# A SwiGLU kernel on one core: x rows 0 to 383 turned by a DMA copy, in place of 256 rows turned on TensorE

## The chip, the cores and the metric

The kernel runs on one core of one Trainium2 chip; the other seven cores are idle. The metric is the device time of one execution in microseconds (us), as the median of several runs. A profile of one execution goes with it: it lists what each engine did and when. The engines are TensorE (PE, with its weight loads as PEld), VectorE (DVE), ScalarE (ACT), GpSimd (POOL) and SyncE (SP). SP and ACT issue the DMA transfers here, each on a queue of its own.

## The reference

```python
B, S, D, F = 1, 2048, 640, 1536          # all bfloat16
def reference(x, w_gate, w_up, w_down):
    g = silu(x @ w_gate)                 # [2048, 1536]
    u = x @ w_up                         # [2048, 1536]
    return (g * u) @ w_down              # [2048, 640]
```

## The kernel before, in words

The 2048 rows of x are worked on in four blocks of 512 (`S_BLK`). A matmul contracts over the 128 partitions, so x has to stand with D on the partitions: `xT` holds it so, as 5 slices (kd) of 128 by 2048. `wg_sb` and `wu_sb` hold the two first weights, also as 5 slices; F is cut into 12 chunks of 128 (fc). For each block and each fc, the gate projection (`pg`) and the up projection (`pu`) are 5 matmuls each of up to 512 columns (`proj`, lines 192 to 203). ACT then takes the silu of `pg`, and DVE multiplies it by `pu` into `aT` (`gate`, lines 210 to 217). After the 12 chunks of a block the down projection follows: 12 matmuls for the last 128 columns of the output, turned back on DVE, and 4 x 12 matmuls for its first 512 columns (lines 258 to 308). The last four rows of x are worked out on DVE, spread over the later blocks, so that the last block has only 508 columns in its projections.

The change touches the head, which is block 0 with the first four fc (`EARLY = 4`). Its loads are issued in program order, and SP's instructions are kept in that order to the end (`keep_order`, line 315). Before:

- SP loads x rows 0 to 127 as they lie, ACT loads rows 128 to 255 (`load_x`, lines 111 and 112).
- The gate weights of the first four fc come in five slices of 128 KB, one for each kd (lines 113 to 117): kd 1 on ACT's queue, the others on SP's.
- Rows 256 to 511 are copied by `turn_x` (line 118), a DMA that turns the data through the crossbar on its way, so that they land in `xT` directly.
- Behind it SP issues the first two `wu_sb` loads of 320 KB (two fc each), then the rest of the gate and up weights, w_down, x rows 512 to 1023 by crossbar and more.

Meanwhile PE runs `N_WARM = 18` matmuls on a tile of ones, whose result isn't used (`warm`, line 174). It then turns the first 256 rows itself: 10 transposes of 128 by 128 against an identity (which POOL makes, line 71), copied out of PSUM by ACT and DVE (`transpose_chunk`, line 180). The gate matmuls of the head (lines 230 to 235) go kd by kd over all four fc, so that each needs only one slice of weights: first kd 0 in two steps of 128 columns, then kd 1 to 4 over columns 0 to 255 (`HALF`), then all five kd over columns 256 to 511. After them the four up projections of the head run, each 5 matmuls of 512 columns. PE's order in the head is fixed as written (line 241).

Of the kernel before, what the change touches and what calls it, by code (L numbers as in the profile page):

```python
# [7 lines left out]


@with_exitstack  # L10
def _body(
# [8 lines left out]
    nc = tc.nc  # L20
    P = nc.NUM_PARTITIONS
    f32 = mybir.dt.float32
    bf16 = mybir.dt.bfloat16
    ACT = mybir.ActivationFunctionType
    ALU = mybir.AluOpType

    B, S0, D = x.shape
    F = w_gate.shape[1]
    S = B * S0
    x2 = x.rearrange("b s d -> (b s) d")  # L30
    out2 = out.rearrange("b s d -> (b s) d")

    KD = D // P
    KF = F // P
    S_BLK = 512
    NSB = S // S_BLK
    SUB = S_BLK // P
    HALF = S_BLK // 2
    DA = 512
    Q = 32  # L40
    N_WARM = 18
    T = 4
    WT_STEP = 4
    ROW_J = 0
    EARLY = 4
# [3 lines left out]
    consts = ctx.enter_context(tc.tile_pool(name="consts", bufs=1))  # L49
    work = ctx.enter_context(tc.tile_pool(name="work", bufs=3))  # L50
    outp = ctx.enter_context(tc.tile_pool(name="outp", bufs=3))
    psum = ctx.enter_context(
        tc.tile_pool(name="psum", bufs=2, space=bass.MemoryType.PSUM)
    )

    ident = consts.tile([P, P], bf16)
    x_sb = consts.tile([P, HALF // P, D], bf16)
    xT = consts.tile([P, KD, S], bf16)
    wg_sb = consts.tile([P, KD, F], bf16)
    wu_sb = consts.tile([P, KD, F], bf16)  # L60
# [7 lines left out]
    row_s = consts.tile([P, KF, T], f32)  # L68
    prod = consts.tile([P, D], f32)

    make_identity(nc, ident[:])

    x_v = x2.rearrange("(c p) d -> p c d", p=P)
    xt_v = x2.rearrange("s (kd p) -> s kd p", p=P)
    wg_v = w_gate.rearrange("(kd p) f -> p kd f", p=P)
    wu_v = w_up.rearrange("(kd p) f -> p kd f", p=P)
# [2 lines left out]
    def wslice(a, b):  # L79
        return slice(a * P, b * P)  # L80

    def load_w(eng, dst, src, a, b):
        eng.dma_start(out=dst[:, :, wslice(a, b)], in_=src[:, :, wslice(a, b)])

    def load_x(eng, c0, c1):
        eng.dma_start(out=x_sb[:, c0:c1, :], in_=x_v[:, c0:c1, :])  # L86

    def issue_order(a, b):
        tc.add_manual_dep(
# [8 lines left out]
    def keep_order(engine):  # L98

        traced = [i for i in nc.cur_bb.bb.instructions if i.engine == engine]  # L100
        for a, b in zip(traced, traced[1:]):
            issue_order(a, b)

    def turn_x(r0, r1):
        nc.sync.dma_start_transpose(out=xT[:, :, r0:r1], in_=xt_v[r0:r1])

    ones = consts.tile([P, P], bf16)
    silu_first = consts.tile([P, 1], f32)
    nc.vector.memset(ones[:], 1.0)  # L109

    load_x(nc.sync, 0, 1)
    load_x(nc.scalar, 1, 2)
    for kd in range(KD):
        eng = nc.scalar if kd == 1 else nc.sync
        eng.dma_start(
            out=wg_sb[:, kd, wslice(0, EARLY)], in_=wg_v[:, kd, wslice(0, EARLY)]
        )
    turn_x(HALF, S_BLK)
    nc.scalar.activation(silu_first[:], ones[:, 0:1], ACT.Silu)  # L119
    for a in range(0, EARLY, 2):  # L120
        load_w(nc.sync, wu_sb, wu_v, a, a + 2)
    for a, b in W_CHUNKS:
# [6 lines left out]
    def turn_w(dst, src, f0, f1):  # L129
# [7 lines left out]
        out=x_row[:],  # L137
        in_=x2[S - T : S, :].rearrange("t d -> (t d)").partition_broadcast(P),
# [35 lines left out]
    def warm(n):  # L174
        for _ in range(n):
            nc.tensor.matmul(  # L176
                pw[:, 0:P], lhsT=ones[:], rhs=ones[:], start=True, stop=True
            )

    def transpose_chunk(c, parts):  # L180
        c_sl = slice(c * P, (c + 1) * P)
        for copy, tag, k0, k1 in parts:
            pt = psum.tile([P, k1 - k0, P], bf16, tag=tag, name="pt")
            for kd in range(k0, k1):
                nc.tensor.transpose(  # L185
                    out=pt[:, kd - k0, :],
                    in_=x_sb[:, c, kd * P : (kd + 1) * P],
                    identity=ident[:],
                )
            copy(out=xT[:, k0:k1, c_sl], in_=pt[:])  # L190

    def proj_step(ps, w_sb, fc, sb, c0, c1, kd):
        nc.tensor.matmul(  # L193
            ps[:, c0:c1],
            lhsT=w_sb[:, kd, fc * P : (fc + 1) * P],
            rhs=xT[:, kd, sb * S_BLK + c0 : sb * S_BLK + c1],
            start=(kd == 0 and c0 in (0, HALF)),
            stop=(kd == KD - 1),
        )

    def proj(ps, w_sb, fc, sb, c0, c1):
        for kd in range(KD):
            proj_step(ps, w_sb, fc, sb, c0, c1, kd)
# [6 lines left out]
    def gate(pg, pu, sb, fc, n_s):  # L210

        s0 = sb * S_BLK
        sg = work.tile([P, S_BLK], f32, name="sg")
        nc.scalar.activation(sg[:, 0:n_s], pg[:, 0:n_s], ACT.Silu)  # L214
        nc.vector.tensor_tensor(  # L215
            out=aT[:, fc, s0 : s0 + n_s], in0=sg[:, 0:n_s], in1=pu[:, 0:n_s], op=ALU.mult
        )

    def head():
        dve, act = nc.vector.tensor_copy, nc.scalar.copy  # L220
        split = [(act, "po_a", 0, 2), (dve, "po_b", 2, KD)]
        pgs = [
            psum.tile([P, S_BLK], f32, tag="gu", name="pg", bufs=4)
            for _ in range(EARLY)
        ]
        warm(N_WARM)
        for c in range(HALF // P):
            transpose_chunk(c, split)

        steps = [(0, 0, P), (0, P, HALF)]  # L230
        steps += [(kd, 0, HALF) for kd in range(1, KD)]
        steps += [(kd, HALF, S_BLK) for kd in range(KD)]
        for kd, c0, c1 in steps:
            for fc in range(EARLY):
                proj_step(pgs[fc], wg_sb, fc, 0, c0, c1, kd)

        for fc in range(EARLY):
            pu = psum.tile([P, S_BLK], f32, tag=("po_a", "po_b")[fc % 2], name="pu")
            proj(pu, wu_sb, fc, 0, 0, S_BLK)
            gate(pgs[fc], pu, 0, fc, S_BLK)  # L240
        keep_order(mybir.EngineType.PE)
        keep_order(mybir.EngineType.Activation)

    head()
    for sb in range(NSB):
        n_s = S_BLK if sb < NSB - 1 else S_BLK - T
# [26 lines left out]
        for q in range(P // Q):  # L273
            nc.scalar.dma_start(
                out=out2[
                    sb * S_BLK : sb * S_BLK + n_t, DA + q * Q : DA + (q + 1) * Q
                ].rearrange("(i r) c -> r i c", r=Q),
                in_=ot_q[q * Q : (q + 1) * Q, :].rearrange("r (i c) -> r i c", c=Q),
            )

        for j in range(SUB):
# [6 lines left out]
            for c0, c1, tag in cols:  # L288
# [14 lines left out]
                eng = nc.sync if c1 < D else nc.scalar  # L303
# [82 lines left out]
def kernel(tc, *args):  # L386
    _body(tc, *args)
    tc.close()
    tc.compile()
    _trim(tc.nc)  # L390
# [30 lines left out]
```

## Time and profile before

| | us |
|---|---|
| median of 3 runs | 163.65 |
| lowest, highest | 163.2, 164.01 |
| span of the profiled execution | 161.8 |
| PE busy in it | 159.4 |
| DVE busy | 111.0 |
| ACT busy | 42.6 |

The span runs from the first to the last instruction of the profiled execution. That execution has no device time of its own listed; the median of the runs is 1.85 us above its span. A row of the timeline gives start, length, engine, line, operation, tiles and count; SPq and ACTq are the queues of the engines that issue DMAs, and the length there is that of issuing, not of the transfer. "To landing" counts from the start of the issue to the last of the transfer's completion marks. A matmul's length in a row includes the time in the pipeline, so the spacing of many is taken instead. A row of windows has, for each engine, busy time and count of instructions, then the granted clock, the busy share of the DMA engines and GB/s.

### The profile page before, as it was taken

Reading aid. Unit: us, or ns where it says so; the run is one execution under the profiler, and the core shown is the slowest. Engines: PE = TensorE matmul, PEld = TensorE weight load, DVE = VectorE, ACT = ScalarE, POOL = GpSimd, SP = SyncE. Lnnn points to the kernel's source line nnn. Section 1 sums busy time; section 2 is a strip of 40 time slices with the busy share of each in tenths; the row PEclk is TensorE's granted clock in tenths of the full one; section 3 lists DMA queues with packets and bytes.
Section 4 is the critical chain, followed back from the end, with each engine's and each line's share of the span. In section 5 each row is a group of like instructions: output and inputs, shape, how many; then the busy total and the mean of one; then the engine's idle time right before and its main releaser. Section 6 shows DMA issues by size and latency. Waiting matters only on the chain.

```text
span 161.8 us, 2142 instructions
## 1 busy us (share of the span) xinstructions
PE 159.4 (99%) x808; PEld 77.6 (48%) x808; DVE 111.0 (69%) x250; ACT 42.6 (26%) x74; POOL 0.6 (0%) x6
## 2 busy tenths in 40 slices
PE   8999999999999999999999999999999999999995
PEld 7854444444444444444444444444444444445454
DVE  2034223599569999989919999979964999993001
ACT  5051222112222222211222322221214222222121
POOL 1000000000000000000000000000000000000000
PEclk9999999999999999999999999999999999999999
DMA  6999999934189999003110000000321000000312
GB/s 212 231 351 349 361 248 231 222 75 91 34 192 159 235 236 184 4 0 34 65 65 0 0 4 2 0 0 3 62 67 34 0 0 0 0 0 4 48 41 73
DMA packets 41961, 15.86 MB, mean 98 GB/s; under 512 B 33504, under 2 KB 41824, under 8 KB 41952
## 3 DMA queue, kind: packets, MB, share of 16 engines
q1 hardware_dynamic: 33584, 14.93, 37.0%
q10 hardware_dynamic: 8368, 0.80, 3.5%
q8 instruction: 6, 0.10, 0.3%
q14 instruction: 3, 0.02, 0.1%
HBM read 6.88 MB, written 2.62 MB: 59 GB/s over the span
## 4 chain that ended last, share of the span: by engine, by line
PE 97%; DMA 2%; SPq 0%; DVE 0%; issue 0%
PE pg L193 32%; PE pu L193 32%; PE po_a L291 26%; PE po_t L261 6%; DMA wg_sb<-in_w_gate_dram 2%; SPq L86 0%; DVE ot_b L302 0%
## 5 line engine op out<-in xcount | busy, mean ns | idle before, releaser
L193 PE MATMUL pg<-xT,wg_sb 128*128 128x512 bf16 (+3 forms) x264 | 59.8, 363 | 0.1
L193 PE MATMUL pu<-xT,wu_sb 128*128 128x512 bf16 (+1 forms) x240 | 59.1, 379 | 0.0
L215 DVE TENSOR_TENSOR aT<-sg,pu 128x512 bf16<-128x512 f32 (+1 forms) x48 | 32.7, 682 | 32.3 <-PE pu L193 32.3
L214 ACT ACTIVATE sg<-pg 128x512 f32<-128x512 f32 (+1 forms) x48 | 28.4, 597 | 71.2 <-PE pg L193 67.4
L291 PE MATMUL po_a<-wd_sb,aT 128*128 128x512 bf16 (+4 forms) x228 | 42.8, 348 | 0.0
L147 DVE SCALAR_TENSOR_TENSOR prod<-wgT,x_row 128x640 f32<-128x640 bf16 x48 | 39.4, 821 | 1.5 <-DMA wgT<-in_w_gate_dram 0.4
L147 DVE SCALAR_TENSOR_TENSOR prod<-wuT,x_row 128x640 f32<-128x640 bf16 x48 | 39.4, 821 | 1.0
L193 PEld LDWEIGHTS <-wg_sb 128*128 128x128 bf16 x264 | 25.9, 100 | 26.8 <-DMA wg_sb<-in_w_gate_dram 0.4
L193 PEld LDWEIGHTS <-wu_sb 128*128 128x128 bf16 x240 | 23.4, 98 | 28.1 <-DMA wu_sb<-in_w_up_dram 0.3
L291 PEld LDWEIGHTS <-aT 128*128 128x128 bf16 x228 | 20.8, 98 | 21.7
L300 ACT CAST ot<-po_a 128x512 bf16<-128x512 f32 (+2 forms) x17 | 9.5, 559 | 31.8 <-PE po_a L291 20.2
L261 PE MATMUL po_t<-aT,wd_sb 128*128 128x512 bf16 (+1 forms) x48 | 10.4, 366 | 0.0
L261 PEld LDWEIGHTS <-wd_sb 128*128 128x128 bf16 x48 | 4.7, 98 | 5.1
L302 DVE CAST ot_b<-po_a 128x96 bf16<-128x96 f32 (+1 forms) x2 | 0.5, 240 | 9.7 <-PE po_a L291 9.6
L270 ACT CAST ot_t<-po_t 128x512 bf16<-128x512 f32 (+1 forms) x4 | 2.2, 559 | 11.6 <-PE po_t L261 11.6
L147 DVE DVE_READ_ACCUMULATOR prod<-wgT,x_row 128x1 f32 x48 | 3.9, 82 | 0.0
L147 DVE DVE_READ_ACCUMULATOR prod<-wuT,x_row 128x1 f32 x48 | 3.9, 82 | 0.0
L272 DVE STREAM_TRANSPOSE ot_q<-ot_t 128x512 bf16<-128x512 bf16 (+1 forms) x4 | 2.7, 676 | 1.7 <-ACT ot_t L270 1.7
L190 DVE COPY xT<-pt 128x384 bf16<-128x384 bf16 x2 | 0.7, 358 | 2.9 <-PE pt L185 2.9
L176 PE MATMUL pw<-ones 128*128 128x128 bf16 x18 | 2.1, 313 | 0.4 <-DVE ones L109 0.4
L176 PEld LDWEIGHTS <-ones 128*128 128x128 bf16 x18 | 1.8, 147 | 0.4 <-DVE ones L109 0.4
L119 ACT ACT_TABLE_LOAD x1 | 1.3, 1283 | 1.0 <-issue 1.0
(13 smaller groups left out, 4.7 us busy)
## 6 DMA issues: line engine op xcount, KB each, us to landing
wd_sb<-in_w_down_dram SPq DMA_DIRECT2D x1, 1920.0 KB, 13.0
out_dram<-ot SPq DMA_DIRECT2D x15, 128.0 KB, 1.7
wg_sb<-in_w_gate_dram SPq DMA_DIRECT2D x2, 640.0 KB, 7.9
wu_sb<-in_w_up_dram SPq DMA_DIRECT2D x2, 640.0 KB, 8.6
wu_sb<-in_w_up_dram SPq DMA_DIRECT2D x2, 320.0 KB, 4.7
x_row<-in_x_dram SPq DMA_DIRECT2D x1, 640.0 KB, 5.1
wg_sb<-in_w_gate_dram SPq DMA_DIRECT2D x4, 128.0 KB, 3.4
out_dram<-ot_q ACTq DMA_DIRECT2D x12, 32.0 KB, 1.9
```

Source lines behind the costliest of these rows:

```text
L119: nc.scalar.activation(silu_first[:], ones[:, 0:1], ACT.Silu)
L147: nc.vector.scalar_tensor_tensor(out=prod[:], in0=wT[:, fc, :], scalar=1.0, in1=x_row[:, t, :], op0=ALU.mult, op1=ALU.mult, accum_out=acc[ ...
L176: nc.tensor.matmul(pw[:, 0:P], lhsT=ones[:], rhs=ones[:], start=True, stop=True)
L190: copy(out=xT[:, k0:k1, c_sl], in_=pt[:])
L193: nc.tensor.matmul(ps[:, c0:c1], lhsT=w_sb[:, kd, fc * P : (fc + 1) * P], rhs=xT[:, kd, sb * S_BLK + c0 : sb * S_BLK + c1], start=(kd == 0 ...
L214: nc.scalar.activation(sg[:, 0:n_s], pg[:, 0:n_s], ACT.Silu)
L215: nc.vector.tensor_tensor(out=aT[:, fc, s0 : s0 + n_s], in0=sg[:, 0:n_s], in1=pu[:, 0:n_s], op=ALU.mult)
L261: nc.tensor.matmul(po_t[:], lhsT=wd_sb[:, kf, DA:D], rhs=aT[:, kf, sb * S_BLK : sb * S_BLK + n_t], start=(kf == 0), stop=(kf == KF - 1),)
L270: nc.scalar.copy(ot_t[:], po_t[:])
L272: nc.vector.transpose(out=ot_q[:], in_=ot_t[:])
L291: nc.tensor.matmul(po[:], lhsT=aT[:, kf, s0 : s0 + P], rhs=wd_sb[:, kf, c0:c1], start=(kf == 0), stop=(kf == KF - 1),)
L300: nc.scalar.copy(ot[:], po[:])
```

## The change

Columns 0 to 383 of `xT` come by one crossbar copy, the very first DMA on SP. The five gate slices follow on SP's queue in three DMAs (kd 0; kd 1 and 2; kd 3 and 4), then the crossbar copy of rows 384 to 511, then the same loads as before. ACT issues no load in the head any more, and its first silu (which loads its table) is written ahead of the loads. The plain x loads, the identity, the transposes and their copies are gone. The head's gate matmuls are 20 of 384 columns and then 20 of 128, and 30 warm-up matmuls run in place of 18.

```diff
-    HALF = S_BLK // 2
+    HALF = 3 * P
-    N_WARM = 18
+    N_WARM = 30
...
-    ident = consts.tile([P, P], bf16)
-    x_sb = consts.tile([P, HALF // P, D], bf16)
...
-    make_identity(nc, ident[:])
...
-    load_x(nc.sync, 0, 1)
-    load_x(nc.scalar, 1, 2)
-    for kd in range(KD):
-        eng = nc.scalar if kd == 1 else nc.sync
+    def load_d(eng, k0, k1):
         eng.dma_start(
-            out=wg_sb[:, kd, wslice(0, EARLY)], in_=wg_v[:, kd, wslice(0, EARLY)]
-        )
+            out=wg_sb[:, k0:k1, wslice(0, EARLY)], in_=wg_v[:, k0:k1, wslice(0, EARLY)]
+        )
+
+    nc.scalar.activation(silu_first[:], ones[:, 0:1], ACT.Silu)
+    turn_x(0, HALF)
+    load_d(nc.sync, 0, 1)
+    load_d(nc.sync, 1, 3)
+    load_d(nc.sync, 3, KD)
     turn_x(HALF, S_BLK)
-    nc.scalar.activation(silu_first[:], ones[:, 0:1], ACT.Silu)
...
-    def transpose_chunk(c, parts):
...
     def head():
-        dve, act = nc.vector.tensor_copy, nc.scalar.copy
-        split = [(act, "po_a", 0, 2), (dve, "po_b", 2, KD)]
...
         warm(N_WARM)
-        for c in range(HALF // P):
-            transpose_chunk(c, split)
-
-        steps = [(0, 0, P), (0, P, HALF)]
-        steps += [(kd, 0, HALF) for kd in range(1, KD)]
+        steps = [(kd, 0, HALF) for kd in range(KD)]
         steps += [(kd, HALF, S_BLK) for kd in range(KD)]
```

More of the change, by code (lines that the diff above doesn't have):

```diff
@@ L6 @@
 from concourse._compat import with_exitstack
-from concourse.masks import make_identity
 @with_exitstack
@@ L69, in _body @@
     prod = consts.tile([P, D], f32)
-    make_identity(nc, ident[:])
-    x_v = x2.rearrange("(c p) d -> p c d", p=P)
     xt_v = x2.rearrange("s (kd p) -> s kd p", p=P)
@@ L83, in load_w @@
         eng.dma_start(out=dst[:, :, wslice(a, b)], in_=src[:, :, wslice(a, b)])
-    def load_x(eng, c0, c1):
-        eng.dma_start(out=x_sb[:, c0:c1, :], in_=x_v[:, c0:c1, :])
     def issue_order(a, b):
@@ L178, in warm @@
             )
-    def transpose_chunk(c, parts):
[L181 to L188, printed above, removed]
-                )
-            copy(out=xT[:, k0:k1, c_sl], in_=pt[:])
     def proj_step(ps, w_sb, fc, sb, c0, c1, kd):
```

## The prediction

> **What bounds the kernel now.** I read the page first, its first lines and its chain.
>
> ```profile
> span 161.8 us, 2142 instructions
> PE 159.4 (99%) x808; PEld 77.6 (48%) x808; DVE 111.0 (69%) x250; ACT 42.6 (26%) x74; POOL 0.6 (0%) x6
> ...
> PEclk9999999999999999999999999999999999999999
> ...
> PE 97%; DMA 2%; SPq 0%; DVE 0%; issue 0%
> ```
>
> TensorE is the bound from its first gate matmul to the end, and 97% of the chain is PE. Only the head, where DMA decides, can move. So next the chain in order of time (start, length, what; the last row is from the far end and serves as a price).
>
> ```profile
> 0.45 3.21 DMA wg_sb<-in_w_gate_dram
> ...
> 3.71 5.21 PE pg L193 x44
> 8.92 4.37 PE pu L193 x20
> 13.29 1.08 PE pg L193 x5
> 14.36 1.08 PE pu L193 x5
> ...
> 43.50 1.08 PE pg L193 x5
> ...
> 146.90 1.95 PE po_t L261 x12
> ```
>
> The first gate matmul starts at 3.71, when gate slice kd 0 has landed (0.45 + 3.21 = 3.66). From there on PE is handed from group to group with no wait in the chain. So the question is one number: when does the first up projection (`pu`) start after the change, and does anything behind it wait for DMA? The timeline gives that start, 8.79 (start, length, instruction, count).
>
> ```profile
> 0.39 2.10 PE L176 MATMUL pw<-ones 128*128 128x128 bf16 x18 [0.39 <-DVE ones L109]
> 2.31 1.25 PE L185 MATMUL pt<-ident,x_sb 128*128 128x128 bf16 x10
> 3.71 5.21 PE L193 MATMUL pg<-xT,wg_sb 128*128 128x128 bf16 x44
> 8.79 4.49 PE L193 MATMUL pu<-xT,wu_sb 128*128 128x512 bf16 x20
> ...
> 14.20 1.24 PE L193 MATMUL pu<-xT,wu_sb 128*128 128x512 bf16 x5
> ```
>
> These rows also price a matmul. Five 512-wide ones take 1.08 us in the chain (216 ns each), twelve 384-wide ones 1.95 (162.5 ns): 53.5 ns per 128 columns, so about 55 ns for 128 and 109 ns for 256. But the 18 warm-up matmuls, 128 wide, take 2.10 us: less some 0.3 for the last one's tail, that is 105 ns each, twice the later price. The first microseconds run at half clock, although the PEclk row shows 9 from the start. The 44 gate matmuls (8 of 128 and 36 of 256) would cost 8 x 55 + 36 x 109 = 4.36 us at the full rate; from 3.71 to 8.79 they took 5.08. Of the 0.72 over, I put about 0.6 down to a cold stretch until roughly 4.9 (1.2 us at half rate); the rest is small waits.
>
> **SP's queue and the landings.** First SP's issues, then landings (us from issue; two answers for single 320 KB and 640 KB loads), then the three copies by crossbar: 256 rows in the head, 512 rows at 44.58 and at 59.73.
>
> ```profile
> 0.00 0.39 SPq L86 DMA_DIRECT2D x_sb<-in_x_dram  x1
> 0.45 1.84 SPq L115 DMA_DIRECT2D wg_sb<-in_w_gate_dram  x4
> 2.33 1.91 SPq L105 DMA_TRANSPOSE xT<-in_x_dram  x1
> 4.29 1.15 SPq L83 DMA_DIRECT2D wu_sb<-in_w_up_dram  x2
> ...
> 6.06 0.92 SPq L83 DMA_DIRECT2D wu_sb<-in_w_up_dram  x1
> ...
> 11.83 11.46 SPq L105 DMA_TRANSPOSE xT<-in_x_dram  x1
> ...
> 44.58 2.73 SPq L105 DMA_TRANSPOSE xT<-in_x_dram  x1
> ...
> 59.73 3.22 SPq L105 DMA_TRANSPOSE xT<-in_x_dram  x1
> ```
>
> ```profile
> DMA to landing us min/median/max: 3.2/3.4/3.6
> ...
> wu_sb<-in_w_up_dram SPq DMA_DIRECT2D x1, 320.0 KB, 4.5
> wu_sb<-in_w_up_dram SPq DMA_DIRECT2D x1, 320.0 KB, 4.9
> wu_sb<-in_w_up_dram SPq DMA_DIRECT2D x1, 640.0 KB, 8.0
> ...
> out_dram<-ot SPq DMA_DIRECT2D x15, 128.0 KB, 1.7
> ```
>
> ```profile
> xT<-in_x_dram SPq DMA_TRANSPOSE x1, 4.2
> ...
> xT<-in_x_dram SPq DMA_TRANSPOSE x1, 5.4
> ...
> xT<-in_x_dram SPq DMA_TRANSPOSE x1, 5.2
> ```
>
> The first row of the second fence is the gate slices (128 KB each). The first `wu` load was issued at 4.29 and landed at 4.29 + 4.5 = 8.8, just when `pu` started: gates and load arrive together today. The 640 KB `wu` load for fc 4 to 7 was issued at 6.06 and landed at 14.0; its first user starts at 14.20. That is a cover of only 0.2 us.
>
> **The change, part by part.**
>
> *Removed.* The 10 transposes (1.25 us of PE), their four copies on DVE and ACT, the identity on POOL, the two plain x loads. All of it lay ahead of 3.71 and beside the gate slice that was waited for until 3.66, so none of it is saved as such. It does take away the PE work that filled 2.31 to 3.56. ACT's queue loses a gate slice, which goes to SP.
>
> *Warm-up, 18 to 30 matmuls.* At 107 ns (0.39 to 2.3 for 18) they are all issued by 0.39 + 30 x 0.107 = 3.6. They cost nothing as long as the first gate can't start before that, and it can't. What matters is the idle time behind them.
>
> *x rows 0-383 by crossbar, first on SP.* No row shows 384. Issue: 256 rows 1.91 us, 512 rows 2.73 to 3.22; I take 2.35. Landing: between 4.2 (256 rows) and 5.4 (512); I take the middle, 4.75. DMA rates give much the same. The windows below (last column GB/s) are plain loads in the head, then the first microsecond and the rest of the 512-row copy issued at 44.58.
>
> ```profile
> 2.00:3.00 1.00, 1.00 (x12) 0.92 (x11) 0.00 (x0) 0.77 (x3) 0.00 (x0) 1.00 0.95 315
> ...
> 45.80:46.80 1.00, 1.00 (x7) 0.41 (x6) 1.00 (x2) 0.02 (x1) 0.00 (x0) 1.00 0.89 165
> 46.80:48.50 1.70, 1.70 (x9) 0.78 (x8) 1.67 (x5) 0.57 (x1) 0.00 (x0) 1.00 1.24 275
> ```
>
> The 384 rows are 492 KB: 1 us at 165 and 1.2 us at 275. The data begin some 1.2 us after the issue (44.58 to 45.8), so they end near 3.4 to 3.6 and the semaphore comes later.
>
> The Trainium skill, page "Advanced Engine Details and Errata", section X-Bar Transpose (TRN2), calls such copies as fast as regular ones, 350 to 400 GB/s; by that figure 492 KB would take an estimated 1.2 to 1.4 us, the copy would land near 4.0 and the sum would fall to about +0.1. The rows just shown, 165 and then 275, speak against it here.
>
> *Gate slices behind it, all on SP.* kd 0 is issued at 2.40 instead of 0.45, kd 1-2 at 2.85, kd 3-4 at 3.4 (about 0.45 to 0.5 each, from 1.84 for four). Landing of kd 0: never sooner than 2.40 + 1.7 = 4.1 (the 128 KB store alone), at the latest 2.40 + 3.6 = 6.0. It lies behind the copy in the queue, and 128 KB at 315 GB/s is 0.4 us: 4.75 + 0.4 = 5.15. The other two have double size: 5.95 and 6.75.
>
> *Gates on 384 columns.* 20 x 162.5 ns = 3.25 and 20 x 55 ns = 1.10: 4.35, the same as the 4.36 above. At full clock: 5.15 + 0.65 = 5.80 (kd 0), wait to 5.95, + 1.30 = 7.25 (kd 1-2), + 1.30 = 8.55 (kd 3-4, landed by 6.75), + 1.10 = 9.65.
>
> *The copy of rows 384-511.* It is issued at 3.95. By the 256-row copy it lands no later than 3.95 + 4.2 = 8.15, and its first user is at 8.55: hidden by the 384-wide gates, cover 0.4. Its issue time is on the path, though: from 256 and 512 rows a straight line gives 1.3 to 1.5; in proportion it would be 1.0. I take 1.45.
>
> *What it is moved past.* The `wu` loads go from 4.29 to 5.45, and all later loads by as much. First `wu` chunk: 5.45 + 4.5 = 9.95 by today's row, 5.45 + 3.4 = 8.85 by the faster slices; today's waits behind a 256-row copy and will wait behind 128, so 4.2: 9.65, as late as the gates. Second chunk 6.0 + 4.9 = 10.9, wanted at 9.7 + 10 x 0.216 = 11.9. The 640 KB load moves with the stream, 14.0 + 0.9 = 14.9, against a use at 14.2 + 0.9 = 15.1: the 0.2 cover holds if DMA loses no more than PE. Behind that DMA has slack (the 512-row copy, issued at 11.83, isn't used before 43.5).
>
> **Sum.** `pu` starts at about 9.7 instead of 8.79: +0.9 us, and everything behind it moves by that. The span is 161.8 and the median of the runs 163.65; I carry the 1.85 between them unchanged: 164.55, say 164.6. Without a clock effect the change starts at +1.44 on the first gate (5.15 against 3.71) and gets about 0.6 back because its gates begin after the cold stretch.
>
> **Rivals.**
>
> *The clock is still cold (slower by more).* Before, PE works without a gap over 0.2 us from 0.39 on. After, it idles from 3.6 to about 5.15. If that gap spoils the release and the 4.5 us of work that preceded it in the old kernel (0.39 to 4.9) have to start again at 5.15, the gates run at half rate until 9.7: 14 of 384 (0.325 each) in that time, then 6 x 0.1625 + 1.10 = 2.1; `pu` at 11.8, +3.0 us, 166.6. If it is released halfway, +1.9. For it: the gap is new and long. Against it: more warm-up lies ahead of it. Chance 0.27.
>
> The Trainium skill, "TensorE: Matmul & The Clock Gate", section What's actually happening, has a free-running window of about 3.4 us that must be busy before the full clock is given; by that rule, with a window that ended near 4.9 in the old run, the same window would be some 60% busy (1.5 to 3.6), and if that is too little the next ends near 8.3: an estimated +2.5 us, 166.1. What share is enough the section doesn't say, and the trace only agrees that the first microseconds are slow.
>
> *Nothing lost (the other side).* Place: the queue behind the crossbar copy. If it lands at 4.2 like 256 rows and kd 0 follows at 4.4, the gates, warm and never waiting, end at 4.4 + 4.35 = 8.75, and `wu` at 8.85 decides: +0.1, 163.7. It decides from a first gate at 4.43 or earlier (8.79 - 4.35). For it: no other load is ahead of the copy now. Against: kd 0 can't pass it, and the 512-row copies took 5.2 and 5.4. Chance 0.20 for -0.4 to +0.5.
>
> *A real gain.* The runs of before spread from 163.2 to 164.0. If this comes from the moment of release, the old cold head may cost more than the 0.6 us of this profile in a typical run, while the new gates escape it. With one more microsecond of cold in the typical old run and the previous rival's landings it is -1 us, 162.7. Chance 0.10.
>
> **How the numbers follow.** The likeliest, 0.43, is +0.5 to +1.4, middle +0.9: 164.6, its own range 164.1 to 165.1. A measurement of this kernel can tell about 0.5% (0.82 us) from no change, and the likeliest lies on that border: 0.29 of its 0.43 above it. Slower: 0.29 + 0.27 = 0.56; same: 0.14 + 0.20 = 0.34; faster 0.10. The range runs from 163.2 (below nothing lost, by the spread) to 166.6 (clock fully lost); it leaves out the gain and a little above.
>
> **What would show it.** In the changed profile: SP's first copy about 2.35 us long and landing at 4.5 to 5; the first gate between 4.9 and 5.4, held by `wg_sb` and not by `xT`; its chain rows 4.35 us long plus a wait below 0.3; `pu` at 9.5 to 10; then a shift that is the same for the groups at 13.29 and 43.50 and at the end. A gate stage of 6 us or more without waits is the cold clock. A first gate under 4.5 is the second rival. Wrong in size: a `wu` load landing well after the gates' end, or a new wait near 15 on the 640 KB load.

## The result and the profile after

| | before | after |
|---|---|---|
| median of the runs | 163.64 us | 165.32 us |
| lowest, highest | 163.2, 165.71 | 163.88, 166.18 |
| span of the profiled execution | 161.8 | 162.6 |

The ratio of after to before is 1.0102, with a 95% interval of 1.0058 to 1.0147: slower by 1.7 us. The medians differ by more than the two profiles do (0.8 us). The profiled execution of after is the quickest of its six (163.88); three of the six lie at 163.9 to 164.7 and three at 165.9 to 166.2, and the median falls between them, where no run lies. So the profile shows one part of the loss only. Three disturbed executions, 165.71 of before and 166.56 and 168.6 of one kernel below, are left out of all ratios.

The page of after, first lines and chain:

```profile
span 162.6 us, 2114 instructions
PE 158.4 (97%) x794; PEld 76.5 (47%) x806; DVE 110.3 (68%) x248; ACT 41.9 (26%) x72; POOL 0.2 (0%) x4
...
PE 95%; DMA 2%; SPq 1%; issue 0%; DVE 0%
```

Its chain in order of time (start, length, what):

```profile
0.00 1.39 SPq L96
...
1.44 3.59 DMA wg_sb<-in_w_gate_dram
...
5.08 4.65 PE pg L174 x40
...
14.05 1.08 PE pg L174 x5
...
44.27 1.08 PE pg L174 x5
```

The chain still runs over the gate slice kd 0, which now is issued at 1.44 and lands at 5.04. The group of block 1 that stood at 43.50 stands at 44.27, 0.77 later. The timeline of after:

```profile
0.00 1.39 SPq L96 DMA_TRANSPOSE xT<-in_x_dram  x1
0.40 3.38 PE L169 MATMUL pw<-ones 128*128 128x128 bf16 x30 [0.40 <-DVE ones L100]
1.44 1.55 SPq L103 DMA_DIRECT2D wg_sb<-in_w_gate_dram  x3
3.04 1.20 SPq L96 DMA_TRANSPOSE xT<-in_x_dram  x1
4.28 1.15 SPq L77 DMA_DIRECT2D wu_sb<-in_w_up_dram  x2
5.08 4.65 PE L174 MATMUL pg<-xT,wg_sb 128*128 128x384 bf16 x40 [1.30 <-DMA wg_sb<-in_w_gate_dram]
9.79 4.26 PE L174 MATMUL pu<-xT,wu_sb 128*128 128x512 bf16 x19
13.89 1.24 PE L174 MATMUL pg<-xT,wg_sb 128*128 128x512 bf16 x5
```

Between the end of the warm-up at 3.78 and the first gate at 5.08, PE does nothing. The `pu` row has 19 matmuls where 20 ran: its first record is missing, and the true start is 13.89 - 20 x 0.216 = 9.57. To be safe from that, I compare kernels by the start of the next group, the gates of fc 4: 13.89 here. In before it is 13.12, by this row of its timeline:

```profile
13.12 1.24 PE L193 MATMUL pg<-xT,wg_sb 128*128 128x512 bf16 x5
```

Landings in after (copy of 384 rows; kd 0; kd 1-2; kd 3-4; copy of 128 rows; first `wu`; us from issue):

```profile
xT<-in_x_dram SPq DMA_TRANSPOSE x1, 4.1
...
wg_sb<-in_w_gate_dram SPq DMA_DIRECT2D x1, 128.0 KB, 3.6
...
wg_sb<-in_w_gate_dram SPq DMA_DIRECT2D x1, 256.0 KB, 3.7
...
wg_sb<-in_w_gate_dram SPq DMA_DIRECT2D x1, 256.0 KB, 4.0
...
xT<-in_x_dram SPq DMA_TRANSPOSE x1, 4.2
...
wu_sb<-in_w_up_dram SPq DMA_DIRECT2D x1, 320.0 KB, 4.2
```

The copy is there at 4.1, kd 0 only at 5.04. Fourteen of the sixteen completion marks of kd 0 came by 4.56, the last two at 4.89 and 5.04.

### The profile page after: what moved, and what is told of

The parts are those of the page before. It is cut to its first block, busy times and chain, and to the rows that moved or that the text cites. A ratio compares the mean times of both kernels' runs of the same rounds, so it can differ in the third digit from the quotient of the medians.

```text
span 162.6 us, 2114 instructions
## 1 busy us (share of the span) xinstructions
PE 158.4 (97%) x794; PEld 76.5 (47%) x806; DVE 110.3 (68%) x248; ACT 41.9 (26%) x72; POOL 0.2 (0%) x4
## 4 chain that ended last, share of the span: by engine, by line
PE 95%; DMA 2%; SPq 1%; issue 0%; DVE 0%
PE pg L174 32%; PE pu L174 32%; PE po_a L266 26%; PE po_t L236 6%; DMA wg_sb<-in_w_gate_dram 2%; SPq L96 1%; DVE ot_b L277 0%
## 5 line engine op out<-in xcount | busy, mean ns | idle before, releaser
L174 PE MATMUL pg<-xT,wg_sb 128*128 128x512 bf16 (+3 forms) x254 | 58.9, 362 | 1.6 <-DMA wg_sb<-in_w_gate_dram 1.3
L174 PEld LDWEIGHTS <-wg_sb 128*128 128x128 bf16 x260 | 24.5, 98 | 28.9 <-DMA wg_sb<-in_w_gate_dram 1.9
L169 PE MATMUL pw<-ones 128*128 128x128 bf16 x30 | 3.4, 313 | 0.4 <-DVE ones L100 0.4
L169 PEld LDWEIGHTS <-ones 128*128 128x128 bf16 x30 | 3.1, 148 | 0.4 <-DVE ones L100 0.4
```

The lines of the kernel that those rows point to most:

```text
L169: nc.tensor.matmul(pw[:, 0:P], lhsT=ones[:], rhs=ones[:], start=True, stop=True)
L174: nc.tensor.matmul(ps[:, c0:c1], lhsT=w_sb[:, kd, fc * P : (fc + 1) * P], rhs=xT[:, kd, sb * S_BLK + c0 : sb * S_BLK + c1], start=(kd == 0 ...
```

## The experiments

Theory: two costs add up. One is the order of the loads, in every execution: the first gate waits for a slice that lies behind the copy. The other is the clock, in some executions only: PE idles ahead of the first gate, and the full clock is then given some 4 us later. The rival to the second part was late transfers. All kernels below start from the changed one, except where the kernel before is named; each ratio is to runs of the kernel before that were made beside the kernel's own. The table gives the start of the gates of fc 4 in the profile, the median and the ratio to before with its interval.

| kernel | fc 4 gates | median | ratio |
|---|---|---|---|
| before | 13.12 | 163.4 to 163.6 | |
| after | 13.89 | 165.32 | 1.0102 (1.0058 to 1.0147) |
| after, again | 15.68 | 165.78 | 1.0141 (1.0119 to 1.0162) |
| 44 warm-up matmuls | 14.11 | 164.14 | 1.0044 (1.0027 to 1.0060) |
| 8 warm-up matmuls | 15.74 | 166.09 | 1.0145 (1.0121 to 1.0168) |
| first copy 256 rows | 15.41 | 165.33 | 1.0100 (1.0062 to 1.0138) |
| kd 0 on ACT | 15.64 | 165.12 | 1.0061 (1.0024 to 1.0097) |
| kd 0 on ACT, 38 warm-up | 13.68 | 163.63 | 1.0011 (0.9998 to 1.0024) |
| the same, kd 1 alone | 13.60 | 163.84 | 1.0017 (0.9998 to 1.0036) |
| kd 0 to 2 on ACT, 38 warm-up | 14.24 | 164.61 | 1.0072 (1.0048 to 1.0097) |
| before with 6 warm-up | 14.29 | 164.36 | 1.0056 (1.0039 to 1.0072) |

**The changed kernel again.** No edit.

> The changed kernel, unaltered, for the spread of its runs. Its six runs so far went from 163.88 to 166.18, three of them at 165.9 to 166.2, while the profiled one, with span 162.6, is the quickest. Theory: the head costs a fixed +0.8 to +1.0 us (first up projection at 9.8 instead of 8.8), and in about half of the executions the full clock comes late on top, another 1.5 to 2.5 us; so the runs fall into two groups, near 164 and near 166. Rival: the upper group comes from late transfers (the first crossbar copy or a gate slice), and PE works at the full clock in it too.

All four runs fell between 165.66 and 166.15, so this time the profile has what the first one lacked. Its timeline, and windows (the third item from the left is PE busy with the count of matmuls):

```profile
0.40 3.38 PE L169 MATMUL pw<-ones 128*128 128x128 bf16 x30 [0.40 <-DVE ones L100]
4.96 6.57 PE L174 MATMUL pg<-xT,wg_sb 128*128 128x384 bf16 x40 [1.18 <-DMA wg_sb<-in_w_gate_dram]
11.36 4.48 PE L174 MATMUL pu<-xT,wu_sb 128*128 128x512 bf16 x20
15.68 1.24 PE L174 MATMUL pg<-xT,wg_sb 128*128 128x512 bf16 x5
```

```profile
5.50:6.50 1.00, 1.00 (x4) 0.46 (x3) 0.00 (x0) 0.00 (x0) 0.00 (x0) 1.00 1.28 179
7.00:8.00 1.00, 1.00 (x5) 0.46 (x4) 0.00 (x0) 0.00 (x0) 0.00 (x0) 1.00 1.11 263
```

The first gate is no later than in the other profile (4.96), and PE waits for nothing behind it. Yet the gates take 6.57 instead of 4.65. Their starts are 320 ns apart until 9.09 and 162 ns apart from 9.27. That is the half clock until about 9.2, and it costs 1.79 us (15.68 against 13.89). (In these profiles starts are 107, 213 and 320 ns apart where the same 128, 256 and 384 columns later take 56, 109 and 162: close to double at each width.) Late transfers as the cause fall: the slices landed within 0.13 us of the other profile's. Nor was it a bad moment of the machine: the twelve runs of the kernel before made beside these four lie between 163.06 and 163.91. The PEclk column says 1.00 in these rows all the same.

**44 warm-up matmuls instead of 30.**

```diff
-    N_WARM = 30
+    N_WARM = 44
```

> 44 warm-up matmuls instead of 30, so that PE is busy from 0.4 until about 5.1 and the idle 1.3 us ahead of the first gate are gone. Clock theory: the upper group vanishes; all runs between 163.8 and 164.6, median near 164.2, spread under 1 us. Transfers as the rival: two groups as without the edit, median 165.3.

Seven runs, 164.10 to 164.42: nothing near 166 is left. The timeline and the same windows:

```profile
0.39 4.79 PE L169 MATMUL pw<-ones 128*128 128x128 bf16 x44 [0.39 <-DVE ones L100]
5.35 4.60 PE L174 MATMUL pg<-xT,wg_sb 128*128 128x384 bf16 x40 [0.17 <-DMA wg_sb<-in_w_gate_dram]
```

```profile
5.50:6.50 1.00, 1.00 (x7) 0.51 (x6) 0.00 (x0) 0.00 (x0) 0.00 (x0) 1.00 1.22 152
7.00:8.00 1.00, 1.00 (x8) 0.59 (x6) 0.00 (x0) 0.00 (x0) 0.00 (x0) 1.00 1.18 262
```

Seven and eight matmuls to the microsecond against four and five. The edit does no useful work; it fills the idle stretch alone. So of the 2.15 us that after, again lost against before (165.78 - 163.63), 1.64 are the clock (165.78 - 164.14), and 0.51 are left for the order of the loads.

**8 warm-up matmuls.**

```diff
-    N_WARM = 30
+    N_WARM = 8
```

> 8 warm-up matmuls instead of 30: PE idles from about 1.4 to 5.1. Clock theory: no execution has the full clock at the first gate; the gates run at half rate for 2 to 4.6 us, so every run lies in or above the upper group, 165.3 to 167, and the profile shows 384-wide gate matmuls at 0.325 us instead of 0.1625. Transfers as the rival: nothing changes, two groups, median 165.3.

All six runs lie between 165.11 and 166.27, all but one of them within the 165.3 to 167 of the clock theory, and the one 0.2 below. The gates:

```profile
0.40 1.03 PE L169 MATMUL pw<-ones 128*128 128x128 bf16 x8 [0.40 <-DVE ones L100]
5.43 6.16 PE L174 MATMUL pg<-xT,wg_sb 128*128 128x384 bf16 x40 [3.99 <-DMA wg_sb<-in_w_gate_dram]
```

The spacing falls from 320 to 163 ns at 8.8. With 8 warm-up matmuls the median is only 0.3 us worse than with 30 (165.78): the 22 more that the change has bought little in the runs beside these. What they did buy is that three of the ten runs with 30 stayed below 165, and none of the six with 8.

**The kernel before with a gap.** 6 warm-up matmuls instead of 18, in the kernel before.

```diff
-    N_WARM = 18
+    N_WARM = 6
```

> The kernel before with 6 warm-up matmuls instead of 18: PE idles from about 1.1 to 2.3, a gap as long as the one that the change brought in, and nothing else differs. Clock theory: the full clock comes later in many executions than at 4.95, and the gates cost up to 1.7 us more: median 164.2 to 165.3 with a wider spread than the 0.85 us of the kernel before. If only the gap right before the first gate counted, or none: 163.6 as before.

```profile
2.43 1.25 PE L185 MATMUL pt<-ident,x_sb 128*128 128x128 bf16 x10
...
3.47 6.66 PE L193 MATMUL pg<-xT,wg_sb 128*128 128x128 bf16 x44
```

The gap of 1.2 us, from 1.2 to 2.4, lies ahead of the transposes here. Some loads land up to 0.6 us later than in the first profile of before (gate slice kd 3 at 5.42 against 4.83), but PE waits for none of them: its starts follow each other without a break from 2.43 to the end of the gates. Still the gates take 6.66 instead of 5.21, with 256-wide matmuls 213 ns apart until 7.74. Median 0.93 us worse, the spread no wider (0.85). So a gap of 1.2 us is enough without anything else of the change, and it need not be right ahead of the gates.

**The kernel before, two more profiles.**

> The kernel before, unaltered, for a second profile of it: its runs lie between 163.1 and 164.3, and the profiled one (span 161.8, full clock at 4.95) was among the quickest. If the moment of the full clock makes that spread, a run with a span of 162.2 or more has gates at half rate past 4.95, and the spacing tells until when: 0.4 us of span for each 0.8 us that it is later. If transfers make it, the clock comes near 4.95 again and a wait for a gate slice or for the up weights is longer.

> The same once more, for a third profile of the kernel before.

Both have a span of 162.3, the common one. Timeline of the first, then of the second:

```profile
3.99 5.46 PE L193 MATMUL pg<-xT,wg_sb 128*128 128x128 bf16 x44 [0.32 <-DMA wg_sb<-in_w_gate_dram]
9.29 4.48 PE L193 MATMUL pu<-xT,wu_sb 128*128 128x512 bf16 x19
```

```profile
6.95 2.34 PE L193 MATMUL pg<-xT,wg_sb 128*128 128x256 bf16 x20 [0.46 <-DMA xT<-in_x_dram]
9.24 4.49 PE L193 MATMUL pu<-xT,wu_sb 128*128 128x512 bf16 x19
```

In the first the full clock comes at about 5.9 and the first slice 0.3 us later than in the profile above. In the second the clock comes at 4.6, but PE waits 0.46 us for the crossbar copy of rows 256 to 511, and then for the up weights. So both causes are in the spread of the kernel before (0.85 us beside the first experiments, 1.04 and 1.12 beside the later ones), and the profile that the prediction was worked from is one of the lucky ones, 0.5 us below the common run. That is why the shift of 1.0 us of the 44-warm-up kernel against that profile (14.11 against 13.12) is only 0.51 in the medians.

**256 rows in the first copy.**

```diff
-    HALF = 3 * P
+    HALF = 2 * P
```

> First crossbar copy of 256 rows instead of 384 (the second one then has 256 too), all else as changed. Head theory (the first gate waits for the gate slice that lies behind the copy in the queue): 164 KB less ahead of the slice is 0.55 us at 290 GB/s, so the first gate starts near 4.5 instead of 5.08, the up projections near 9.3 or later if the second copy, now larger, is waited for; quick runs 0.2 to 0.5 us below those of the unaltered changed kernel. Rival: the slice's last completion marks are late by themselves (two of its sixteen came 0.3 to 0.5 us after the others), whatever lies ahead: first gate still at 5.0.

The copy's landing and the first gate:

```profile
xT<-in_x_dram SPq DMA_TRANSPOSE x1, 3.5
```

```profile
4.86 6.40 PE L174 MATMUL pg<-xT,wg_sb 128*128 128x256 bf16 x40 [1.08 <-DMA wg_sb<-in_w_gate_dram]
```

The copy lands 0.6 us earlier, the slice behind it only 0.2 us: nearer the rival's 5.0 than my 4.5. The first of the slice's completion marks came 0.64 us earlier, in step with the copy (3.76 against 4.40), the last one 0.22 (4.82 against 5.04). So the late marks follow the bytes ahead of the slice only in part, as far as one profile of each can tell. Runs from 164.11 to 166.19, the two groups as before, so nothing is gained; the profiled run has the half clock until about 8.7.

**kd 0 on ACT's queue, with 38 and with 30 warm-up matmuls.** The edit of the kernel with 30; the other has `N_WARM = 38` besides.

```diff
+    load_d(nc.scalar, 0, 1)
     nc.scalar.activation(silu_first[:], ones[:, 0:1], ACT.Silu)
     turn_x(0, HALF)
-    load_d(nc.sync, 0, 1)
     load_d(nc.sync, 1, 3)
```

> From the changed kernel: gate slice kd 0 goes to ACT's queue as its first instruction, instead of behind the crossbar copy on SP's, and 38 warm-up matmuls (until about 4.45). Theory that the first gate waits for the slice because it lies behind the copy: the slice lands before 4, the first gate starts at the copy's landing, 4.3 to 4.5, then waits for slices kd 1 and 2, which come at 5.5 to 5.8 as before; first up projection 9.2 to 9.5, median 163.6 to 164.0 (0.3 to 0.5 below the 44-warm-up kernel). Rival, that the bytes ahead of the first gate decide whatever their order: the copy lands later by what the slice takes, first gate 4.9 to 5.1, nothing gained, 164.1.

> The changed kernel with only the place of slice kd 0 altered (ACT's queue), 30 warm-up matmuls as in the change; with the two kernels of 44 and 38 it makes a square of the two causes. The first gate starts near 4.4, so the idle stretch ahead of it is 0.6 to 0.8 us instead of 1.2 to 1.6, and another of about 0.4 to 0.7 follows before kd 1. Clock theory: some executions still get the full clock late, median between 163.7 and 165.3, lower than the changed kernel's 165.3 to 165.8. If the two causes were one (the order alone): 163.6 with a spread as small as with 38.

With 38, twelve runs of 163.41 to 164.14: level with the kernel before. Timeline with 38, then with 30:

```profile
4.42 0.81 PE L174 MATMUL pg<-xT,wg_sb 128*128 128x384 bf16 x4
...
5.64 3.89 PE L174 MATMUL pg<-xT,wg_sb 128*128 128x384 bf16 x36 [0.41 <-DMA wg_sb<-in_w_gate_dram]
...
13.68 1.24 PE L174 MATMUL pg<-xT,wg_sb 128*128 128x512 bf16 x5
```

```profile
0.39 3.38 PE L169 MATMUL pw<-ones 128*128 128x128 bf16 x30 [0.39 <-DVE ones L100]
4.49 7.00 PE L174 MATMUL pg<-xT,wg_sb 128*128 128x384 bf16 x40 [0.72 <-DMA xT<-in_x_dram]
```

The first gate comes 0.6 us sooner, as the order theory said; then kd 1 is waited for, so that the gain is smaller. With 30, the idle stretch is only 0.72 us (a second one, ahead of kd 1, is 0.09 by the spacing), and the runs still fall into two groups: five at 163.5 to 163.9, seven at 165.0 to 165.9. The profiled one has the half clock until 9.5. So the square reads, as loss against before in us: 2.15 (neither cured), 0.51 (gap filled), 1.60 (order alone; 165.12 - 163.52), 0.20 (both). Filling the gap is worth 1.4 to 1.6, the order 0.3 to 0.55, and with both nothing measurable is left of the loss.

**kd 0 to 2 on ACT.** With `N_WARM = 38` besides.

```diff
+    load_d(nc.scalar, 0, 1)
+    load_d(nc.scalar, 1, 3)
     nc.scalar.activation(silu_first[:], ones[:, 0:1], ACT.Silu)
     turn_x(0, HALF)
-    load_d(nc.sync, 0, 1)
-    load_d(nc.sync, 1, 3)
```

> As the former, with slices kd 1 and 2 on ACT's queue too, so that 393 KB of slices move in the stretch in which the crossbar copy alone used 200 GB/s. Order theory: first gate 4.4 to 4.6, no wait behind it, gates until 8.8 to 9.0, up load landed by then as SP reaches it earlier; first up projection near 8.9, median 163.0 to 163.5, below the kernel before. Bytes theory: copy lands at 4.8 or later, first gate 4.9 to 5.1, first up projection 9.3 to 9.5, 163.8.

The copy's landing with kd 0 alone beside it, then with kd 0 to 2:

```profile
xT<-in_x_dram SPq DMA_TRANSPOSE x1, 4.2
```

```profile
xT<-in_x_dram SPq DMA_TRANSPOSE x1, 5.5
```

The bytes theory comes out right, and by more than its numbers: 256 KB more beside the copy cost it 1.3 us between these two profiles, and the first gate came at 5.56. The runs in the table lie at 164.1 to 165.1. The gates:

```profile
5.56 4.53 PE L174 MATMUL pg<-xT,wg_sb 128*128 128x384 bf16 x40 [1.29 <-DMA xT<-in_x_dram]
```

Here the spacing of the warm-up matmuls falls from 107 to 56 ns at 3.75. PE then idles for 1.29 us, as long as in the changed kernel, yet all gates are 162 ns apart from the first on. So in this profile a gap behind the moment of the full clock cost no clock; the gaps that did lay ahead of it.

**kd 1 and kd 2 apart.** From the kernel with kd 0 on ACT and 38 warm-up matmuls.

```diff
-    load_d(nc.sync, 1, 3)
+    load_d(nc.sync, 1, 2)
+    load_d(nc.sync, 2, 3)
```

> From the kernel with kd 0 on ACT's queue and 38 warm-up matmuls: slices kd 1 and kd 2 as two DMAs of 128 KB instead of one of 256 KB, for one issue more on SP (0.46 us, all behind it later by that). If the wait of 0.4 us ahead of kd 1 there comes from its sharing a DMA with kd 2, kd 1 lands near 5.0, the gates run from 4.4 to 8.8 without a wait, and the first up projection starts at 8.9 to 9.3, when its weights land: 163.2 to 163.4, a little below the kernel before. If the late last completion marks decide, kd 1 lands at 5.4 or later and nothing is gained: 163.6.

In its profile 13 of the 16 marks of kd 1 were there at 5.05, and the last at 5.51: the marks decide, and nothing is gained (163.84 against 163.63). No kernel here beats the one before.

## Why the prediction was right or wrong

*The sign and the range* held: slower, 165.32 within 163.2 to 166.6, +1.7 us where +0.9 was forecast as likeliest; the likeliest case's own range, 164.1 to 165.1, was missed by 0.2. The size of +1.7 is luck: it is the middle of three runs of an upper group and three of a lower one, and the four further runs, all in the upper one, give +2.15.

*The likeliest case was a part of the whole.* Its "+0.9" is the head at full clock, and the profile of that head came within 0.2 of it: first gate 5.08 (forecast 5.15), held by `wg_sb` and not `xT`, gates of 4.65 us, `pu` at 9.57 (9.7). Against common runs of before it is worth 0.5, since the sum was made against a profile 0.5 us below them. That slip stands in the step "I carry the 1.85 between them unchanged", which sets the median of several runs against the span of one quicker execution. Every run on record that lists both took 1.26 to 1.39 more than its own span. With 1.3 the same sum gives 161.8 + 0.9 + 1.3 = 164.0, and the executions without the late clock were there: 163.88 for the profiled one, 164.14 for 44 warm-up matmuls.

*The mis-sized term is the clock's chance.* "The clock is still cold" was a rival with 0.27. In the ten runs of after, seven are above 165.6, and the one of them that was profiled shows exactly this. It was priced, with the head's own loss, at +3.0, or +1.9 if released halfway; measured, the two together come to 2.15 in the medians, and to 2.56 between the late profile and the one that the prediction was worked from (15.68 against 13.12). The clock's part is 1.6 in the medians (1.79 between two profiles). The prediction's "+2.5" comes to +2.3 when its own terms are added up (half rate from 5.15 to 8.3). The step that failed is "Against it: more warm-up lies ahead of it". More warm-up that ends early is worth little: 8 and 30 matmuls differ by 0.3 us, 30 and 44 by 1.6. Why three of the ten escaped, no run here shows; the chance should have been nearer 0.7 than 0.27.

*Issue times were wrong.* "I take 2.35" for the copy was 1.39, and 1.45 for the second copy was 1.20. The first 256-row copy of the 256-row experiment took 1.34, its second one, behind three gate slices, 2.22, where the 128 rows of the change took 1.20: as the first DMA the issue hardly depends on size (1.34 and 1.39), behind other loads it does, and the 1.91 of the old profile was such an issue. So "the `wu` loads go from 4.29 to 5.45" was wrong, they were issued at 4.28. (The sum didn't follow that step through either: by 1.16 later, the 640 KB load would have landed at 15.2, past its use at 15.1.) The copy landed at 4.1 instead of 4.75. It made no difference, as kd 0's landing took 3.6 us from issue instead of the 2.75 that I worked out, which cancelled the earlier issue. So the first gate's nearness to the forecast, 5.08 against 5.15, is luck: the slice followed the copy by 0.46 for fourteen of its marks, as forecast (0.4), but the last two took 0.5 more, a term that the sum doesn't have.

*The rates of the copy* came as the old rows said. In after:

```profile
1.30:2.30 1.00, 1.00 (x13) 1.00 (x11) 0.00 (x0) 0.31 (x2) 0.00 (x0) 1.00 0.92 176
2.30:3.30 1.00, 1.00 (x12) 1.00 (x11) 0.00 (x0) 0.00 (x0) 0.00 (x0) 1.00 1.28 291
```

176 GB/s and then 291, against 165 and 275. The 350 to 400 GB/s of the Trainium skill ("Advanced Engine Details and Errata", section X-Bar Transpose (TRN2)) don't show here either. The landing near 4.0 that was worked out from that figure was close all the same (4.1), but the first gate wasn't waiting for the copy, it was waiting for the slice behind it.

*Nothing lost* needed a first gate by 4.43. It took kd 0 on the other queue to get one at 4.42. *Covers*: the second copy landed at 7.2, before its use at 8.45, and the 640 KB load at 14.17 against 14.97; both held.

## What to carry to other kernels

Filling idle TensorE time ahead of the first real work pays up to the moment that this work can start, not for a fixed count: when a first load moves later, the filler has to grow with it. In seven of twelve runs 0.7 us of gap was enough to lose some 1.5 us. It is the gap ahead of the full clock that costs; behind it, 1.3 us cost none in the one profile that has such a gap. A head that is lucky in one profile has to be judged by its runs; where they form two groups, look at the spacing of the matmuls in one profile of each. A load that the first work waits for should not be queued behind another that it doesn't depend on; that was worth 0.3 to 0.55 us here.

## What the runs showed that I had not expected

The full clock comes at very different times from the same start: by the spacing of matmuls at 3.3 (kd 1 alone), 3.75 (kd 0 to 2 on ACT), 4.6, 4.95 and 5.9 (kernel before), and at 7.8, 8.7, 8.8, 9.2 and 9.5 in kernels with a gap. That is an early group and a late one, with nothing seen between 5.9 and 7.8. (In the three other profiles it came about where the warm-up ends and the gates begin, and can't be read so closely.)

The Trainium skill, "TensorE: Matmul & The Clock Gate", section What's actually happening, explains such a pattern by a free-running window of about 3.4 us that has to be busy. By that rule the kernel with kd 0 on ACT and 30 warm-up matmuls missed a window that ended near 6.1, some 70% of which was busy by the spacing of its matmuls; so an estimate by this page is that more than 70% is wanted. The runs agree with the pattern, but none shows the windows themselves.

A plain load on ACT's queue beside the crossbar copy of 384 rows delays that copy by about its bytes. Alone the copy landed at 4.1 (four profiles), with 128 KB beside it at 4.2, 4.4 and 4.6, with 384 KB at 5.5; at the 291 GB/s seen above, an estimate for the delay is 0.45 and 1.35 us. And the last one to three of a load's sixteen completion marks were often 0.2 to 0.5 us behind the rest, for the slices that the first gates wait for.
